# Two exponential tiles in one ScalarE instruction, 17 joint maximum units for 14, and six edits of the ending, in a fused attention and GEGLU kernel

## The chip, the cores and the metric

One core of a Trainium2 chip runs the whole program. The metric is the device time of one execution in microseconds (us); three runs of the kernel before gave 1225.08 us in the median (1224.64 to 1225.44). In the views, PE is TensorE (PEld its weight loads), DVE VectorE, ACT ScalarE, POOL GpSimd, and SP (SyncE) issues the DMAs.

## What is computed

A transformer block without masks on one sequence, inputs and output in bf16: S = 2048 tokens, D = 512 channels, H = 32 heads of 16 channels, and a feed-forward width F = 1792.

```python
def attn(x, wqkv, wo):
    q, k, v = split(x @ wqkv)                      # 32 heads of 16
    p = softmax(einsum("bhqd,bhkd->bhqk", q, k) * 16 ** -0.5)
    return merge(einsum("bhqk,bhkd->bhqd", p, v)) @ wo

def ffn(x, w_gate, w_up, w_down):
    return (gelu_tanh(x @ w_gate) * (x @ w_up)) @ w_down

h  = x + attn(layernorm(x), wqkv, wo)
h2 = h + ffn(layernorm(h), w_gate, w_up, w_down)   # the output
```

The softmax is over 32 x 2048 x 2048 scores, 134 million of them. Each must be seen twice: once for the maximum of its row, once for its exponential.

## The kernel before, in words

**Units and ticks.** The attention is cut into 64 units. A unit is 4 heads by 256 queries by all 2048 keys, and takes 16 ticks of the main loop. Each tick has a part of *pass 1* for one unit and a part of *pass 2* for the unit 24 ticks behind it (`P2_START`):

- Pass 1 (`p1_pair`, L852; `p1_consume`, L867 or L864): PE writes a pair of score tiles, 128 queries by 512 keys each, into two neighbouring PSUM banks; DVE takes the row maxima of both in one reduce. Four banks, 0 to 3, serve pass 1 as two pairs in turn, so a pair can be written again when the maximum of two ticks before has ended. At a unit's end POOL negates and splits the maxima, a transposing DMA turns them, and POOL adds them to the queries (L922), so that the scores of pass 2 come out with the maximum subtracted.
- Pass 2 (`p2_tile`, L943; `p2_consume`, L972): PE computes the scores again, transposed (keys by queries, 128 x 512 numbers a tile), two tiles a tick, and ACT takes the exponential of each into one of 34 SBUF slots. The slots lie in three tensors, PTM (23), PTE (4) and PTG (7), and are used in turn.

**The PSUM banks of pass 2.** Banks 4 to 7 are handed out by the class `Banks`: a list of free banks, from which `take` pops the first and to which `give` appends. A bank is given back as soon as the instruction that reads it has been planned, so the list is in the order of last use and `take` returns the bank whose reader is oldest. What still has to be awaited on the chip is settled by semaphores.

**Dense items.** All other matrix work is cut into items that run as Python generators: PV products (`item_pv`, L989, at the end of which L696 copies the 128x256 result to OB), projections, gate and up products, down products (`item_down`, L1391), and the difference tiles of the joint units. The class `Dense` lets one item run at a time. It holds one bank from its first piece to its last and yields between the pieces, so one piece is planned per tick, behind the two pass 2 tiles; where no piece fits, a dummy matmul (L1587) keeps PE going. The bank is given back when the item ends.

**Plan and order.** Nothing is scheduled by the hardware or by a compiler: `Plan` records each engine's instructions in program order and puts in semaphore waits from the reads and writes. `act_lag` is an estimate of how far ACT has fallen behind, to which each planned instruction adds; items start, and GELU polynomials and tanhs are placed, by that estimate and by another for POOL (`PoolStream`).

**The group.** In each tick the pass 1 pair and the first tile of pass 2 are wrapped in `group_begin` and `group_end`. The latter gathers the waits of all matmuls in between and puts them in front of the first one:

```python
        for i in range(i0, len(e.ops)):
            fn, waits, sig, dsem = e.ops[i]
            allw.extend(waits)
            e.ops[i] = (fn, [], sig, dsem)
```

So the pass 1 matmuls also wait for the reader of the bank that the first pass 2 tile is to take. The second tile stands outside the group and has its own wait.

**Joint units.** In 14 of the 64 units (`JOINT`) one tick of pass 1 is left out. For two heads, PE makes the difference of two key blocks' scores in one bank (`item_diff`: two accumulating matmuls), ACT writes its Relu to SBUF (L1080), and at tick 10 of the unit two DVE instructions (L864: add the Relu to the scores, take the row maximum) give the joint maximum of both blocks. At tick 14 the loop skips the tick (`J_GONE`); `behind` then counts the two pass 2 tiles that are owed, and the next two odd ticks take a third tile each (`more`).

**The ending.** Once pass 1 is over (`dve_free`), pass 2 runs in double exponentials (`p2_pair`, L960), two per pair of ticks, while the copies of dense items go to DVE. The last group of tokens has its own path: `item_oprojA` and `item_hnA` (output projection and second layer norm of its first half), `item_raw` (gate and up products of that half, copied raw), and `tail_b`, straight-line code for the last PV product, the norm, GELU, down products and the output DMA.

Of the kernel before, what the change touches and what calls it, by code (L numbers as in the profile page):

```python
# [209 lines left out]
ACT = mybir.ActivationFunctionType  # L210
# [5 lines left out]
NFC = F // 128  # L216
# [5 lines left out]
PV_T = (15, 16, 17, 18)  # L222
PV_TL = (9, 10, 17, 18)
DOWN_AT = 2
A_LATE = True
GH = 6
# [11 lines left out]
SLOPE = 0.02  # L238
JOINT = (5, 9, 12, 14, 17, 20, 25, 28, 33, 36, 41, 44, 49, 60)
J_AT, J_GONE = 10, 14  # L240
LAG_EXTRA = 0.3
POLY = 1.3
TICK = 1.135
# [4 lines left out]
def bass_sequential_preLN__mha_block__geglu_ffn__prompt_kernel(nc, A_x, A_wqkv, A_wo, B_x, B_w_gate, B_w_up, B_w_down, out):  # L248
    dbg = None
    with ExitStack() as es:  # L250
# [288 lines left out]
        class Dense:  # L539
            def __init__(self):  # L540
                self.prio = []
                self.ready = []
                self.extra = []
                self.gen = None
                self.bank = None
# [21 lines left out]
            def piece(self):  # L567
                if self.single and self.pause > 0:
                    return 0
                while True:  # L570
# [17 lines left out]
                    try:  # L588
                        cost = next(self.gen)
                        if isinstance(cost, tuple):  # L590
                            if self.single:
                                self.pause = cost[1]
                            if ticking[0]:
                                return 0
                            continue
                        return cost
                    except StopIteration as fin:
                        self.gen = None
                        self.done += 1
                        if self.single:  # L600
                            banks.give(self.bank)
                            self.pause = 0 if dve_free[0] else PAUSE
                        return fin.value
            def busy(self):
                return bool(self.gen is not None or self.ready or self.prio)
# [342 lines left out]
        def p2_pair(ui, tiles):  # L948
# [12 lines left out]
            else:  # L961
                for b, pi in ((b0, q0), (b1, q1)):
                    P.op("act", lambda e, b=b, pi=pi: e.activation(out=PTt(pi), in_=pbank[:, b, :], func=ACT.Exp), reads=[("pb", b)], writes=[("PT", pi)])

        def p2_consume(ui, tiles):
            for (b, m, g) in tiles:
                pi = pt_n[0] % NPT; pt_n[0] += 1
                assert pi not in pt_busy, "PT ring too small"
                pt_busy.add(pi)
                pt_of[(ui, m, g)] = pi  # L970
                dX = rdeps("M", [(n_, i_) for n_ in ("QKE", "QKE2") for i_ in range(5)]) if NPT_M - 10 <= pi < NPT_M else rdeps("E", [("xn", t) for t in range(NT)]) if NPT_M <= pi < NPT_M + NPT_E else (rdeps("G", [("x", cc) for cc in range(NCH)]) if pi >= NPT_M + NPT_E else ())
                P.op("act", lambda e, b=b, pi=pi: e.activation(out=PTt(pi), in_=pbank[:, b, :], func=ACT.Exp), reads=[("pb", b)], writes=[("PT", pi)], extra_deps=dX)  # L972
                banks.give(b)
# [216 lines left out]
        def item_oprojA(b):  # L1190
# [7 lines left out]
            P.op("pe", lambda e: e.matmul(pbank[:, b, :], ident[:], hh, start=False, stop=True), reads=["ident", ("h", GL % 2, 0)], writes=[("pb", b)], sig=True)  # L1198
            P.op("dve", lambda e: e.bn_stats(out=stats2[:, t, :], in_=pbank[:, b, :]), reads=[("pb", b)], writes=[("stats2", t)])
            P.op("dve", lambda e: e.tensor_copy(out=hh, in_=pbank[:, b, :]), reads=[("pb", b)], writes=[("h", GL % 2, 0)])  # L1200
            P.op("dve", lambda e: e.bn_aggr(out=mv2[:, t, :], in_=stats2[:, t, :]), reads=[("stats2", t)], writes=[("mv2", t)])
            P.op("dve", lambda e: e.tensor_scalar(out=rstd2[:, tt], in0=mv2[:, tt, 1], scalar1=EPS, scalar2=None, op0=ALU.add), reads=[("mv2", t)], writes=[("rstd2", t)])
# [7 lines left out]
        def item_hnA(b):  # L1210
            pt = pbank[:, b, :].bitcast(BF16)
            for dc in range(4):
                P.op("pe", lambda e, dc=dc: e.transpose(out=pt[:, 128 * dc:128 * dc + 128], in_=hn_sb[:, 0, 128 * dc:128 * dc + 128], identity=ident[:]),
                     reads=[("OH", 0), "ident"], writes=[("pb", b)], sig=(dc == 3))
            P.op("dve", lambda e: e.tensor_copy(out=hnT_l[GL % 2][:, :, 0:128], in_=pt[:, 0:512].rearrange("p (c s) -> p c s", c=4)), reads=[("pb", b)], writes=[("hnT", GL % 2, 0)])
            add_raw()
            return 1
            yield
# [299 lines left out]
        def tail_b():  # L1518
# [7 lines left out]
            for t in range(NTL):  # L1526
                raw_gelu(t)
            raw_mult(0)
            while not a_done[0]:
                fill(1)  # L1530
# [12 lines left out]
            P.op("pool", lambda e: e.tensor_tensor(out=rstd2[:, tt], in0=rstd2[:, tt], in1=nhalf[:, 0:1], op=ALU.pow), reads=[("rstd2", t1), "nhalf"], writes=[("rstd2", t1)])  # L1543
            raw_mult(1, "dve")
            raw_mult(2)
            raw_mult(3)
            P.op("dve", lambda e: e.tensor_scalar(out=hn_sb[:, 1, :], in0=g_h(GL, 1), scalar1=mv2[:, t1, 0:1], scalar2=rstd2[:, tt], op0=ALU.subtract, op1=ALU.mult),
                 reads=[("h", 1, 1), ("mv2", t1), ("rstd2", t1)], writes=[("OH", 1)])
            down_h(0, GL, 0)
            for fc in chunks(0):  # L1550
                down_mm(0, GL, 0, fc)
            fill(FILL_A)
            tail_hnT(2, (0, 1), "act")
            tail_hnT(3, (2, 3), "dve")
            for fc in chunks(1):
                down_mm(0, GL, 0, fc)
# [6 lines left out]
            for t in range(NTL):  # L1563
                tail_gate(gb[2 * t % 5], t)
                tail_up(gb[(2 * t + 1) % 5], t)
                if t == 0:
                    for fc in range(8, NFC):
                        down_mm(0, GL, 0, fc)
                    P.op("act", lambda e: e.activation(out=out_sb[:, 0, :], in_=pbank[:, 0, :], func=ACT.Copy), reads=[("pb", 0)], writes=[("osb", 0)])
                    P.dma("sp", lambda e: e.dma_start(out=outv[:, 2 * GL, :], in_=out_sb[:, 0, :]), ("out", 0), reads=[("osb", 0)], writes=[("outd", 2 * GL)])  # L1570
# [33 lines left out]
        ticking[0] = True  # L1604
        def next_tile():
            n = 2 * t2 - behind[0]
            st, jj = n // 2, n % 2
            ui_ = st // 16
            t = p2_tile(ui_, st % 16, 1 - (st + P2_START) % 2, jj)
            return ui_, t  # L1610
        while True:
# [62 lines left out]
            if t1:  # L1674
# [83 lines left out]
```

## Time and profile before

The page is of one profiled execution.

| | us |
|---|---|
| median of three runs | 1225.08 (1224.64 to 1225.44) |
| the profiled execution | 1225.74, its span 1224.0 |
| PE busy | 1130.3 (92%) |
| DVE busy | 1181.1 (96%), 1124 instructions |
| ACT busy | 1190.3 (97%), 2421 instructions |
| POOL busy | 841.3 (69%) |
| L867, maxima on DVE | 996 instructions, 1134.9 |
| L972, exponentials on ACT | 2000 instructions (PTM 1357, PTG 407, PTE 236), 1098.4 |
| L1587, dummy matmuls | 774, 237.0 |
| granted TensorE clock | full speed in all 40 slices |
| HBM read, written | 11.80 MB, 2.10 MB |

How to read it: an engine's busy time is the sum of its instructions' durations, and a duration can be longer than the distance to the next instruction of the same engine, since the end of one overlaps the start of the next. So the distance from start to start in an unbroken run is the price of an instruction, not its mean duration. A busy PE says little here: it runs dummies where it has nothing to do. A group's "idle before" is the time that its engine stood still just ahead of its instructions, with what ended most of it; in the page, the tile of a group is named by the program's names without numbers, so the banks are all "pbank".

In the views by window, a row has the stretch (us from the span's start), then the busy time of PE, of PEld with its count, of DVE, ACT and POOL, then the granted clock, the DMA share and the GB/s. In the chain of what ended last, a row has the start, the duration, the engine and the tile and line. In the time line, a row is one instruction with its start and duration, and in brackets the idle time of its engine ahead of it with what ended it.

### The profile page before, as it was taken

The numbers are of one execution on the slowest core, as the hardware profiler recorded it, in microseconds if no ns is written. First come the engines' busy times: TensorE is split into PE (matmuls) and PEld (weight loads), VectorE is DVE, ScalarE is ACT, GpSimd is POOL, SyncE is SP. The second block draws the span as 40 slices with busy tenths as digits, with TensorE's granted clock in tenths as the row PEclk, the third lists the DMA queues.
The fourth block names the chain that finished last, engine by engine and source line by source line (L and its number), as shares of the span: only waits on it lengthen the run. The fifth ranks groups of instructions, "written<-read, shape, count | busy, mean of one in ns | idle before, by whom it ended". The sixth has DMA issues, their size and how long they took to land.

```text
span 1224.0 us, 36091 instructions
## 1 busy us (share of the span) xinstructions
PE 1130.3 (92%) x14845; PEld 476.7 (39%) x14845; DVE 1181.1 (96%) x1124; ACT 1190.3 (97%) x2421; POOL 841.3 (69%) x1774
## 2 busy tenths in 40 slices
PE   7999998899999999999999999999999999999998
PEld 3233232233333333333332333333334455554565
DVE  8999999999999999999999999999999999999963
ACT  7899999999999999999999999999999999999995
POOL 8567684766776676756868487675767687756762
PEclk9999999999999999999999999999999999999999
DMA  5111104300010000110011000100001100010000
GB/s 153 28 34 27 29 24 136 91 10 9 8 28 21 12 11 8 27 25 8 11 25 14 21 8 10 25 21 15 8 10 27 26 20 13 10 27 13 18 20 15
DMA packets 69651, 32.02 MB, mean 26 GB/s; under 512 B 54768, under 2 KB 68464, under 8 KB 69488
## 3 DMA queue, kind: packets, MB, share of 16 engines
q1 hardware_dynamic: 69488, 29.71, 10.0%
q8 instruction: 118, 1.93, 0.7%
q14 instruction: 45, 0.37, 0.1%
HBM read 11.80 MB, written 2.10 MB: 11 GB/s over the span
## 4 chain that ended last, share of the span: by engine, by line
ACT 56%; DVE 32%; PE 8%; issue 2%; DMA 1%; POOL 1%; POOLq 0%; DVEq 0%
ACT PTM L972 32%; DVE PM L867 31%; ACT PTG L972 10%; ACT PTE L972 5%; PE pbank L1391 2%; ACT th_sb L1262 2%; ACT g_sb L696 2%; ACT u_sb L696 2%; PE pbank L943 1%; PE pbank L852 1%; ACT PTM L960 1%; ACT OB L696 1%; PE pbank L1292 1%; PE pbank L1587 1%; DVE OA L864 1%
## 5 line engine op out<-in xcount | busy, mean ns | idle before, releaser
L867 DVE TENSOR_REDUCE PM<-pbank 128x2 f32<-128x1024 f32 x996 | 1134.9, 1213 | 9.3 <-PE pbank L943 4.4
L972 ACT ACTIVATE PTM<-pbank 128x512 bf16<-128x512 f32 x1357 | 733.0, 718 | 4.4 <-PE pbank L943 1.0
L943 PE MATMUL pbank<-QT,KT 32*128 32x256 bf16 (+1 forms) x5120 | 506.2, 250 | 14.6 <-ACT PTM L972 8.1
L852 PE MATMUL pbank<-KT,QT 32*128 32x512 bf16 x2020 | 388.2, 384 | 25.4 <-DVE PM L867 10.0
L1587 PE MATMUL pbank<-ones_bf,ident 128*128 128x512 bf16 x774 | 237.0, 384 | 29.2 <-ACT PTM L972 4.7
L852 PEld LDWEIGHTS pbank<-KT,QT 32*128 32x128 bf16 x2020 | 97.2, 91 | 351.1 <-DVE PM L867 130.2
L943 PEld LDWEIGHTS pbank<-QT,KT 32*128 32x128 bf16 x5120 | 205.9, 92 | 69.0 <-ACT PTM L972 40.1
L972 ACT ACTIVATE PTG<-pbank 128x512 bf16<-128x512 f32 x407 | 225.1, 710 | 0.8 <-PE pbank L943 0.4
L972 ACT ACTIVATE PTE<-pbank 128x512 bf16<-128x512 f32 x236 | 140.3, 719 | 1.0 <-PE pbank L943 0.7
L989 PE MATMUL pbank<-PTM,VA 128*17 128x256 bf16 (+1 forms) x3470 | 126.0, 252 | 1.6
L1030 POOL TENSOR_TENSOR LINV<-OBT,negone 128x8 f32<-128x8 bf16 x63 | 105.1, 1668 | 6.2 <-DMA OBT<-OB 5.9
L1587 PEld LDWEIGHTS pbank<-ones_bf,ident 128*128 128x128 bf16 x774 | 45.3, 97 | 132.6 <-ACT PTM L972 83.8
L1272 POOL TENSOR_TENSOR th_sb<-g_sb 128x512 f32<-128x512 f32 (+1 forms) x50 | 51.2, 1024 | 63.6 <-ACT g_sb L696 63.6
L989 PEld LDWEIGHTS pbank<-PTM,VA 128*17 128x17 bf16 x3470 | 67.1, 90 | 39.8 <-issue 22.1
L1271 POOL TENSOR_TENSOR th_sb<-th_sb,g_sb 128x512 f32<-128x512 f32 (+1 forms) x50 | 62.4, 1248 | 4.0
L922 POOL TENSOR_TENSOR QT<-QT,STG 128x256 bf16<-128x256 bf16 x64 | 42.8, 668 | 31.8 <-DMA STG<-ST 31.1
L1274 POOL TENSOR_TENSOR th_sb<-th_sb,g_sb 128x512 f32<-128x512 f32 (+1 forms) x50 | 62.3, 1246 | 1.7
L1270 POOL TENSOR_SCALAR th_sb<-th_sb 128x512 f32<-128x512 f32 (+1 forms) x50 | 30.5, 611 | 40.9 <-ACT th_sb L1262 40.7
L1391 PE MATMUL pbank<-wd_sb,GUT 128*128 128x512 bf16 x210 | 57.4, 382 | 1.0 <-DVE OnT L1422 0.3
L767 POOL TENSOR_SCALAR QT<-QKS,qmask 128x512 bf16<-128x512 bf16 x30 | 46.9, 1568 | 13.3 <-ACT QKS L696 11.9
L1347 PE MATMUL pbank<-hnT_l,wg_sb 128*128 128x256 bf16 x336 | 51.2, 275 | 3.3 <-ACT PTM L972 0.7
L1383 POOL TENSOR_TENSOR GUT<-th_sb,u_sb 128x512 bf16<-128x512 f32 x42 | 53.3, 1268 | 1.3
(198 smaller groups left out, 1210.1 us busy)
## 6 DMA issues: line engine op xcount, KB each, us to landing
QKS<-QKS SPq DMA_DIRECT2D x27, 112.0 KB, 2.1
x_sb<-in_A_x_dram SPq DMA_DIRECT2D x4, 512.0 KB, 5.8
xres<-in_A_x_dram SPq DMA_DIRECT2D x16, 128.0 KB, 2.4
out_dram<-out_sb SPq DMA_DIRECT2D x15, 128.0 KB, 1.7
wg_sb<-in_B_w_gate_dram SPq DMA_DIRECT2D x4, 448.0 KB, 4.2
wu_sb<-in_B_w_up_dram SPq DMA_DIRECT2D x4, 448.0 KB, 3.9
wd_sb<-in_B_w_down_dram SPq DMA_DIRECT2D x3, 512.0 KB, 4.5
STG<-ST SPq DMA_TRANSPOSE x64, 2.3
```

Of the source, the lines that this page charges most:

```text
L696: P.op("act", lambda e: e.activation(out=o_ap, in_=i_ap, func=ACT.Copy, **kw), reads=reads, writes=writes, extra_deps=extra)
L852: P.op("pe", lambda e, g=g, b=b: e.matmul(pbank[:, b, :], QT[32 * g:32 * g + 32, c, slot, 128 * qt:128 * qt + 128], KT[32 * g:32 * g + 32, ...
L867: P.op("dve", lambda e: e.tensor_reduce(out=PM[:, par, qt, kc, g:g + 2], in_=pbank[:, b:b + 2, :], axis=AX.X, op=ALU.max), reads=[("pb", b ...
L943: P.op("pe", lambda e, kt=kt, i=i: e.matmul(pbank[:, b, qn * i:qn * i + qn], KT[32 * g:32 * g + 32, slot, 128 * kt:128 * kt + 128], QT[32 ...
L972: P.op("act", lambda e, b=b, pi=pi: e.activation(out=PTt(pi), in_=pbank[:, b, :], func=ACT.Exp), reads=[("pb", b)], writes=[("PT", pi)], e ...
L989: P.op("pe", lambda e, g=g, kt=kt, pi=pi, i=i, s_=s_, c0=c0, qn=qn: e.matmul(pbank[32 * g:32 * g + 17, b, c0:c0 + qn], VA[:, kt, 4 * s_ + ...
L1030: P.op("pool", lambda e: e.tensor_tensor(out=li, in0=o4[:, :, :, 16], in1=negone[:, 0:4 * nq].rearrange("p (q h) -> p q h", q=nq), op=ALU. ...
L1271: o(1.27, lambda e: e.tensor_tensor(out=ts_, in0=ts_, in1=gs, op=ALU.mult), [("th", par), ("g", par)])], then=done)
L1274: o(1.27, lambda e: e.tensor_tensor(out=ts_, in0=ts_, in1=gs, op=ALU.mult), [("th", par), ("g", par)])], then=poly_done)
L1383: P.op("pool", lambda e: e.tensor_tensor(out=o_ap, in0=shp(ts_), in1=shp(us), op=ALU.mult), reads=[("th", par), ("u", par)], writes=o_keys ...
L1391: P.op("pe", lambda e: e.matmul(pbank[:, b, :], GUT[:, fc, 128 * k:128 * k + 128], wd_sb[:, fc, :], start=first, stop=last), reads=[("GUT" ...
L1587: P.op("pe", lambda e: e.matmul(pbank[:, b, :], ident[:], ones_bf[:, 0:512], start=True, stop=True), reads=["ident", "ones_bf"], writes=[( ...
```

## The change

**In the loop.** Ahead of the group, `pair_banks` looks for the first bank in the free list whose neighbour (4 with 5, 6 with 7) is free as well. It is called only where pass 1 and pass 2 both run and no dense item holds a bank. If there is one, the two tiles of the tick go into these two banks, the lower one first, in place of the two banks at the head of the list. `p2_both` then makes one ACT instruction over both banks (1024 numbers a partition), if the next two slots are neighbours in the same SBUF tensor; if not, two single ones. A third tile is as before. Each pair takes 0.05 off the estimate `act_lag`.

**Joint units.** Units 22, 30 and 39 join the list.

**Around the end of the loop.** Once pass 1 is over (`dve_free`), an item that has to wait lets another one run beside it in a second bank (`beside`, `under`). Two of the four due times of the last unit's PV pieces go from 17 and 18 to 14 and 17 (counted from its first tick), one more dense piece is planned behind the loop (`TAIL_P`), the raw items are added a tick later, and the statistics of the first half of the last tokens are taken from the bf16 copy in SBUF, behind that copy, in place of PSUM.

**In `tail_b`.** Of the four products of raw gate and up, number 1 goes from DVE to POOL and ahead of the wait for the last attention output, number 2 from POOL to DVE, and number 3 from POOL to DVE behind the transposed copies. Of the 14 down products of the first half, 8 stand ahead of those copies in place of 4, then 4 in place of 4, and 2 in place of 6 behind the first gate and up products.

```diff
-PV_TL = (9, 10, 17, 18)
+PV_TL = (9, 10, 14, 17)
+TAIL_P = 1
-JOINT = (5, 9, 12, 14, 17, 20, 25, 28, 33, 36, 41, 44, 49, 60)
+JOINT = (5, 9, 12, 14, 17, 20, 22, 25, 28, 30, 33, 36, 39, 41, 44, 49, 60)
+PAIR_GAIN = 0.05
...
                         if isinstance(cost, tuple):
+                            if dve_free[0]:
+                                other_cost = self.beside()
+                                if other_cost:
+                                    return other_cost
...
+            def beside(self):
+                if self.under is None:
+                    if not self.ready or not banks.free or self.ready[0][3] > self.now or not startable(self.ready[0], 99):
+                        return 0
+                    genfn, a, est, nb = self.ready.pop(0)
+                    b = banks.take()
+                    self.under = (genfn(b, *a), b, genfn)
+                try:
+                    cost = next(self.under[0])
+                    return 0 if isinstance(cost, tuple) else cost
...
+        def pair_banks():
+            for b in banks.free:
+                if b ^ 1 in banks.free:
+                    return b & 6
+            return None
+
+        def p2_both(tl):
+            (ua, (b0, ma, ga)), (ub, (b1, mb, gb)) = tl
+            n = pt_n[0] % NPT
+            if n + 1 < NPT and pt_tiles[n][0] is pt_tiles[n + 1][0] and b1 == b0 + 1:
+                (q0, d0), (q1, d1) = place(ua, ma, ga), place(ub, mb, gb)
+                o_ap = pt_tiles[q0][0][:, pt_tiles[q0][1]:pt_tiles[q0][1] + 2, :]
+                P.op("act", lambda e: e.activation(out=o_ap, in_=pbank[:, b0:b0 + 2, :], func=ACT.Exp), reads=[("pb", b0), ("pb", b1)], writes=[("PT", q0), ("PT", q1)], extra_deps=d0 + d1)
+                banks.give(b0)
+                banks.give(b1)
+                act_lag[0] = max(0.0, act_lag[0] - PAIR_GAIN)
+            else:
+                for u_, t_ in tl:
+                    p2_consume(u_, [t_])
...
-            P.op("dve", lambda e: e.bn_stats(out=stats2[:, t, :], in_=pbank[:, b, :]), reads=[("pb", b)], writes=[("stats2", t)])
             P.op("dve", lambda e: e.tensor_copy(out=hh, in_=pbank[:, b, :]), reads=[("pb", b)], writes=[("h", GL % 2, 0)])
+            P.op("dve", lambda e: e.bn_stats(out=stats2[:, t, :], in_=hh), reads=[("h", GL % 2, 0)], writes=[("stats2", t)])
...
-            add_raw()
+            defer(1, add_raw)
...
             raw_mult(0)
+            raw_mult(1)
...
-            raw_mult(1, "dve")
-            raw_mult(2)
-            raw_mult(3)
+            raw_mult(2, "dve")
...
-            for fc in chunks(0):
+            for fc in range(8):
                 down_mm(0, GL, 0, fc)
...
             tail_hnT(3, (2, 3), "dve")
-            for fc in chunks(1):
+            raw_mult(3, "dve")
+            for fc in chunks(2):
                 down_mm(0, GL, 0, fc)
...
-                    for fc in range(8, NFC):
+                    for fc in chunks(3):
                         down_mm(0, GL, 0, fc)
...
-        def next_tile():
+        def next_tile(bank=None):
...
-            t2l = [next_tile()] if p2_ok and p1_ok else []
+            pb_ = pair_banks() if p2_ok and p1_ok and dense.gen is None and True else None
+            t2l = [next_tile(pb_)] if p2_ok and p1_ok else []
             P.group_end("pe")
             if p2_ok and p1_ok:
                 behind[0] -= 1
-                t2l.append(next_tile())
+                t2l.append(next_tile(None if pb_ is None else pb_ + 1))
...
+            if pb_ is not None:
+                p2_both(t2l[:2])
+                t2l = t2l[2:]
             for ui_, t in t2l:
                 p2_consume(ui_, [t])
...
+        for _ in range(TAIL_P):
+            dense.pause = 0
+            dense.piece()
```

The slots' bookkeeping of `p2_consume` (ring position, regions that have to be retired first) moves to a helper, `place`, unchanged.

More of the change, by code (lines that the diff above doesn't have):

```diff
@@ L544, in __init__ @@
                 self.gen = None
+                self.under = None
                 self.bank = None
@@ L599, in piece @@
                         self.done += 1
+                        ended = self.bank
+                        if self.under is not None:
+                            self.gen, self.bank, self.cur = self.under
+                            self.under = None
                         if self.single:
-                            banks.give(self.bank)
+                            banks.give(ended)
                             self.pause = 0 if dve_free[0] else PAUSE
                         return fin.value
+            def beside(self):
[8 more added lines that the diff above has]
+                    return 0 if isinstance(cost, tuple) else cost
+                except StopIteration as fin:
+                    banks.give(self.under[1])
+                    self.under = None
+                    return fin.value
             def busy(self):
@@ L963, in p2_pair, with place @@
                     P.op("act", lambda e, b=b, pi=pi: e.activation(out=PTt(pi), in_=pbank[:, b, :], func=ACT.Exp), reads=[("pb", b)], writes=[("PT", pi)])
+        def place(ui, m, g):
+            pi = pt_n[0] % NPT; pt_n[0] += 1
+            assert pi not in pt_busy, "PT ring too small"
+            pt_busy.add(pi)
+            pt_of[(ui, m, g)] = pi
+            dX = rdeps("M", [(n_, i_) for n_ in ("QKE", "QKE2") for i_ in range(5)]) if NPT_M - 10 <= pi < NPT_M else rdeps("E", [("xn", t) for t in range(NT)]) if NPT_M <= pi < NPT_M + NPT_E else (rdeps("G", [("x", cc) for cc in range(NCH)]) if pi >= NPT_M + NPT_E else ())
+            return pi, list(dX)
+        def pair_banks():
[16 more added lines that the diff above has]
+                    p2_consume(u_, [t_])
         def p2_consume(ui, tiles):
             for (b, m, g) in tiles:
[L967 to L971, printed above, removed]
+                pi, dX = place(ui, m, g)
                 P.op("act", lambda e, b=b, pi=pi: e.activation(out=PTt(pi), in_=pbank[:, b, :], func=ACT.Exp), reads=[("pb", b)], writes=[("PT", pi)], extra_deps=dX)
@@ L1608, in next_tile @@
             ui_ = st // 16
-            t = p2_tile(ui_, st % 16, 1 - (st + P2_START) % 2, jj)
+            if bank is not None:
+                banks.free.remove(bank)
+            t = p2_tile(ui_, st % 16, 1 - (st + P2_START) % 2, jj, bank)
             return ui_, t
```

## The prediction

> **What bounds the kernel now.** I read the page's busy times first, then the windows by 100 us, then the chain that ended last, then the time line of a few ticks. A tick is one pass of the main loop: one maximum on DVE, two exponentials on ACT.
>
> The page (columns: busy, share, instructions) and two of its groups:
> ```profile
> PE 1130.3 (92%) x14845; PEld 476.7 (39%) x14845; DVE 1181.1 (96%) x1124; ACT 1190.3 (97%) x2421; POOL 841.3 (69%) x1774
> ...
> L867 DVE TENSOR_REDUCE PM<-pbank 128x2 f32<-128x1024 f32 x996 | 1134.9, 1213 | 9.3 <-PE pbank L943 4.4
> L972 ACT ACTIVATE PTM<-pbank 128x512 bf16<-128x512 f32 x1357 | 733.0, 718 | 4.4 <-PE pbank L943 1.0
> ```
> One window of the middle (busy us of PE, PEld, DVE, ACT, POOL):
> ```profile
> 500.00:600.00 100.00, 93.15 (x1041) 34.25 (x1041) 99.61 (x91) 99.25 (x205) 70.14 (x161) 1.00 0.06 14
> ```
> DVE and ACT are both full. The chain of the ending changes hands between them, and its unbroken runs give each one's step:
> ```profile
> 645.74 34.01 DVE PM L867 x30
> 679.75 0.60 DVE OA L864
> 680.36 0.60 DVE OA L864
> ```
> ```profile
> 872.65 5.91 ACT PTM L972 x12
> ```
> ```profile
> 1198.09 3.67 ACT PTM L960 x4
> ```
> A maximum steps 34.01/30, less the last record's tail, 1.13 us; an exponential 5.91/12 = 0.49; a double one 3.67/4 = 0.92 (0.06 less than two singles). A joint step, two L864, takes 1.22 in place of two maxima, 2.26.
>
> What matters most here is how a tick hangs together where nobody is behind. Time line (start, duration):
> ```profile
> 1176.10 0.39 PE L852 MATMUL pbank<-KT,QT 32*128 32x512 bf16 x2
> ...
> 1176.53 1.23 DVE L867 TENSOR_REDUCE PM<-pbank 128x2 f32<-128x1024 f32 x1 [0.23 <-PE pbank L943]
> 1176.59 0.60 ACT L972 ACTIVATE PTE<-pbank 128x512 bf16<-128x512 f32 x1 [0.16 <-PE pbank L943]
> ...
> 1177.81 0.23 PEld L943 LDWEIGHTS pbank<-QT,KT 32*128 32x128 bf16 x8 [0.38 <-DVE PM L867]
> ```
> From the start of PE's group (G) the maximum starts after 0.43 and the first exponential after 0.49; an exponential alone takes 0.60, a double one alone 1.04 (mean 1074 ns over 15, less for the undisturbed). The maximum ends at 1177.76 and PE goes on at 1177.81: a release costs 0.05. The maxima need a group every 1.13. A group may start when the maximum two ticks back has ended, so it can be early by 1.13 - 0.08 (records overlap) - 0.05 - 0.43 = **0.57 us of slack**; what is later than that stops DVE. Two groups stand as close as 0.87 here:
> ```profile
> 500.94 0.39 PE L852 MATMUL pbank<-KT,QT 32*128 32x512 bf16 x2
> ...
> 501.81 0.39 PE L852 MATMUL pbank<-KT,QT 32*128 32x512 bf16 x2
> ```
> so 0.26 of lost slack comes back in a tick.
>
> **The change, part by part.**
>
> *Double exponentials.* In the built program's order 540 L972 pairs of the loop become one instruction each: 540 x 0.06 = 34 us less work for ACT. What this can give is capped by DVE: 996 x 1.13, 14 joint steps x 1.22 and some 3.5 us of early statistics fill all but 15 us between its first maximum (14.9) and its last (1177.8). Some 1.7 of these lie before 36 us, 1.0 at 895 behind a transposing DMA; 11.5 remain that a quicker ACT could remove (ends: 0 and 13).
>
> *Three more joint units.* 3 x (2.26 - 1.22) = 3.1 us less on DVE, and 6 Relus x 0.49 = 2.9 more on ACT.
>
> *The banks.* Before, the two tiles of a tick take the oldest free banks. Now, where no item holds a bank, `pair_banks` takes the first free bank **together with its neighbour, however recently that was used**. The wait of the first tile stands in front of the whole PE group (`group_end` moves it there), so the two P1 matmuls behind it, and through them DVE, wait for ACT as well. Counting in the built order which ACT instruction each of these groups waits for: before, at least two newer ones always stand behind it (313 times two, 274 three, five four; else a wait already met). After, 265 have one, and **134 wait for the newest of all**: ACT then runs empty while PE fills banks. 62 of them follow the tick "exp, exp, OB" (end of a unit's product, L696), 33 a difference tile's Relu (L1080), 33 a third tile's exponential in a joint unit, 6 others. A difference tile shows why: at its tick it takes the oldest bank, 4, and gives it back; the next pair takes the now oldest, 5, and with it 4.
>
> The price of such a tick, group to group: ACT start 0.49 + double 1.04 + Relu or third tile 0.49 + release 0.05 = 2.07; with OB 0.49 + 0.60 + 0.49 + 0.28 + 0.05 = 1.91. Against 1.13, with full slack, DVE loses 2.07 - 1.13 - 0.57 = 0.37 and 1.91 - 1.13 - 0.57 = 0.21; with none left 0.94. Two ticks after another such one: ACT 0.49 + 1.04 + 0.92 + 0.49, release 0.05, makes 2.99 against 2.26: 0.73. Four after: between 0.27 and 0.84, by whether slack is left; I take 0.55. By their distances in the order: 62 x 0.21 = 13.0; 20 directly behind another x 0.94 = 18.8; 21 two behind x 0.73 = 15.3; 18 four behind x 0.55 = 9.9; 7 apart and 6 others x 0.37 = 4.8. **Sum 62 us.** Ends: 134 all apart, 40; all but OB without slack, 81. Such a stretch is not in the trace of before; the nearest rows are those above.
>
> A second count, by ACT alone: from 66 to 1177.6 us its instructions, each at its step, make 1093 of 1112 us. After: 1093 - 33 + 3 = 1063; each empty stretch costs 0.05 + 0.49 + 0.12 (a double one alone against in a row) = 0.66, and 125 of them lie there: 82, so 1145. Thus 33 us longer even if ACT never idled otherwise. The truth lies above, as ordinary ticks (0.92 of 1.13) idle too.
>
> *The ending.* 24 double exponentials stay, 1178.0 to 1201.8; a half tanh (0.3) leaves them, and idle 0.40 and 0.48 before two may shrink as two L685 copies leave DVE. Then:
> ```profile
> 1203.30 0.29 DVE L685 COPY OA<-pbank 128x128 f32<-128x128 f32 x1 [0.33 <-PE pbank L989]
> ...
> 1207.87 1.27 DVE L1547 TENSOR_SCALAR OnT<-xres,mv,rstd 128x512 bf16<-128x512 bf16 x1 [0.52 <-POOL rstd L1543]
> ```
> The last product no longer stands behind the down item: the OA copy comes some 1.0 earlier. But POOL's second L1490 now stands ahead of its pow, to 1203.87 + 2 x 1.27 = 1206.41 (before: pow from 1206.82), so only 0.4 survives. L1547 ran beside L1490 on POOL; its twin L1204, alone, took 0.41, so 0.86 is gained. PE then does 9 down products (0.22 each) in place of 4 ahead of the gate, and 2 in place of 6 later: 0.4 lost, with the moved residual product. Net 0.9, and 0.4 from the stretch before: 1.3 (ends 0 and 3). The output's DMA on SP follows the same instructions. The swap of L1199 and L1200, the tick's delay of the raw items and the delayed tail items are covered by these doubles on ACT; uncovered they are some 0.7 us. BN from bf16 SBUF adds nothing (L395, 0.68, against 0.70).
>
> *Sum.* Against the profiled execution, 1225.74 us (span 1224.0): - 3.1 - 11.5 - 1.3 + 62 = +46, so 1271.8. The median shown is 0.66 below the profiled one: **1271 us**.
>
> **The rivals.**
> 1. The forecast, 1271: chance 0.72.
> 2. The waits lose only what each loses alone, 40 us, and all old stalls go (13), the ending gives 3: 1225 - 3 - 13 - 3 + 40 = 1246. For it: old stalls and new ones may fall together. Against: 41 of 72 waits of the joint units stand one or two ticks behind another. Chance 0.14.
> 3. **Faster**: the waits find ACT ahead and cost nothing, and DVE alone sets the pace: 1225.1 - 3.1 - 11.5 - 1.3 = 1209. Place: the 134 groups; it decides below 16/134 = 0.12 us for each. For it: ACT has 34 us less to do, and both engines share the chain now. Against: ACT cannot be ahead of tiles that wait for its newest instruction. But the slack is read from one undisturbed tick, and one half larger would cover the most frequent kind. Chance 0.12.
>    [...]
> 4. The change hardly pairs (rings and banks seldom fit) and little moves: 1224, within 0.2%. The built order shows the 540 doubles; chance 0.02.
>
> [...]
>
> **How the numbers follow.** Low end: rival 2, less 6 us if other slack meets a sixth of its 40, 1240. High end: all 72 without slack, 68, OB 13, old stalls halved: 1225 - 3 - 6 + 81 + 1 = 1298. Faster by over 0.2% (about what a measurement here can tell from no change) 0.12, within 0.02, slower 0.86.
>
> **What would show it.** DVE's idle before L892 (now L867) far above 9.3, released by PE; waits of the P1 weight load (L877) for ACT, on instructions of the new double line, OB and OA, in place of those for DVE; ACT busy well below 97%; 990 maxima and 34 joint steps; joint units longer than plain ones by some 2 to 3 us. Wrong, if DVE's busy share in the middle stays at 99%: then rival 3. If the groups of L877 do wait and DVE doesn't, the slack is mis-sized.

## The result and the profile after

The changed kernel takes **1404.34 us** in the median (1399.46 to 1406.66, 4 runs) against 1225.26 before: a ratio of 1.145, 95% interval 1.1435 to 1.1469. It is slower by 179 us, where 46 were forecast. The profiled execution took 1404.33 us, its span 1402.6.

The page of the changed kernel, the rows that answer to those of before (busy times, the granted clock by slices, and the maxima and exponentials with the idle time ahead of them):
```profile
PE 1124.8 (80%) x14694; PEld 463.1 (33%) x14840; DVE 1205.2 (86%) x1128; ACT 1224.5 (87%) x1890; POOL 844.0 (60%) x1779
...
PEclk9999999989999999899988999999999999999999
...
L892 DVE TENSOR_REDUCE PM<-pbank 128x2 f32<-128x1024 f32 x990 | 1155.6, 1218 | 164.0 <-PE pbank L968 157.7
...
L1010 ACT ACTIVATE PTM<-pbank 128x1024 bf16<-128x1024 f32 x398 | 395.8, 1023 | 73.4 <-PE pbank L968 67.1
L1021 ACT ACTIVATE PTM<-pbank 128x512 bf16<-128x512 f32 x561 | 310.7, 597 | 33.8 <-PE pbank L968 31.6
```
The maxima waited 9.3 us before and 164.0 now, nearly all for PE. ACT, full before, waits for PE as well, and PE itself fell from 92% to 80%. Three engines wait for one another, and none is full. Here is the same window of the middle as before:
```profile
500.00:600.00 100.00, 80.61 (x897) 28.38 (x905) 85.33 (x76) 85.85 (x132) 62.55 (x136) 0.90 0.06 14
```
DVE does 76 instructions in it in place of 91, ACT is busy 85.85 in place of 99.25, and the granted clock is 0.90 where it was 1.00.

What PE's pass 1 group waits for, in the waits of the changed kernel (us in total, times, longest):
```profile
PEld pbank L877 <- ACT PTM L1021: 89.2, 137, 1.5
...
PEld pbank L877 <- ACT OB L721: 69.2, 62, 1.6
...
PEld pbank L877 <- ACT OA L1129: 34.9, 33, 1.2
PEld pbank L877 <- ACT PTG L1021: 32.0, 50, 1.4
...
PEld pbank L877 <- ACT PTE L1021: 18.0, 30, 1.6
```
The 62 waits for OB and the 33 for a difference's Relu (written to OA) are the ones that the prediction counted, to the number. Of the 217 behind a single exponential (137, 50 and 30, by the tensor that it writes) it had priced only the 33 third tiles of the joint units.

Laid out along DVE's records: from the first maximum to the end of the last 1162.8 us before and 1342.9 now, so the loop lost 180.1; from there to the end 46.2 before and 44.9 now. Of the 180.1, 154.8 are more idle time ahead of maxima; the rest is mainly the 0.08 us by which two records in a row overlap, lost at 311 more maxima (25), less the 3.1 of the joint units.

### The profile page after: what moved, and what is told of

Read it like the earlier page. It is cut to its first block, busy times and chain, and to the rows that moved or that the text cites. A ratio compares the mean times of both kernels' runs of the same rounds, so it can differ in the third digit from the quotient of the medians.

```text
span 1402.6 us, 35383 instructions
## 1 busy us (share of the span) xinstructions
PE 1124.8 (80%) x14694; PEld 463.1 (33%) x14840; DVE 1205.2 (86%) x1128; ACT 1224.5 (87%) x1890; POOL 844.0 (60%) x1779
## 4 chain that ended last, share of the span: by engine, by line
ACT 58%; PE 35%; issue 3%; DVE 3%; DMA 0%; POOL 0%
ACT PTM L1010 19%; ACT PTM L1021 15%; PE pbank L968 10%; PE pbank L877 10%; ACT PTG L1021 6%; ACT PTG L1010 5%; PE pbank L1636 5%; ACT PTE L1021 4%; PE pbank L1038 3%; PE pbank L1440 3%; ACT PTE L1010 2%; PE pbank L1396 2%; DVE PM L892 2%; ACT th_sb L1311 2%; ACT OB L721 1%
## 5 line engine op out<-in xcount | busy, mean ns | idle before, releaser
L892 DVE TENSOR_REDUCE PM<-pbank 128x2 f32<-128x1024 f32 x990 | 1155.6, 1218 | 164.0 <-PE pbank L968 157.7
L877 PE MATMUL pbank<-KT,QT 32*128 32x512 bf16 x2014 | 401.4, 399 | 150.7 <-ACT OB L721 53.0
L1010 ACT ACTIVATE PTM<-pbank 128x1024 bf16<-128x1024 f32 x398 | 395.8, 1023 | 73.4 <-PE pbank L968 67.1
L1021 ACT ACTIVATE PTM<-pbank 128x512 bf16<-128x512 f32 x561 | 310.7, 597 | 33.8 <-PE pbank L968 31.6
L1636 PE MATMUL pbank<-ones_bf,ident 128*128 128x512 bf16 x650 | 218.0, 406 | 44.5 <-ACT PTM L1010 23.6
L968 PEld LDWEIGHTS pbank<-QT,KT 32*128 32x128 bf16 x5120 | 189.5, 93 | 110.7 <-ACT PTM L1010 60.6
L1010 ACT ACTIVATE PTG<-pbank 128x1024 bf16<-128x1024 f32 x102 | 102.8, 1025 | 22.7 <-PE pbank L968 20.7
L1021 ACT ACTIVATE PTG<-pbank 128x512 bf16<-128x512 f32 x203 | 113.6, 598 | 6.3 <-PE pbank L968 5.7
L1321 POOL TENSOR_TENSOR th_sb<-g_sb 128x512 f32<-128x512 f32 (+1 forms) x50 | 51.2, 1024 | 97.7 <-ACT g_sb L721 97.7
L1021 ACT ACTIVATE PTE<-pbank 128x512 bf16<-128x512 f32 x156 | 89.1, 599 | 7.7 <-PE pbank L968 7.2
L920 POOL TENSOR_TENSOR MX<-PM,MX 128x8 f32<-128x8 f32 x64 | 12.9, 202 | 82.5 <-DVE PM L892 81.7
```

What stands on the lines that cost most here:

```text
L877: P.op("pe", lambda e, g=g, b=b: e.matmul(pbank[:, b, :], QT[32 * g:32 * g + 32, c, slot, 128 * qt:128 * qt + 128], KT[32 * g:32 * g + 32, ...
L892: P.op("dve", lambda e: e.tensor_reduce(out=PM[:, par, qt, kc, g:g + 2], in_=pbank[:, b:b + 2, :], axis=AX.X, op=ALU.max), reads=[("pb", b ...
L968: P.op("pe", lambda e, kt=kt, i=i: e.matmul(pbank[:, b, qn * i:qn * i + qn], KT[32 * g:32 * g + 32, slot, 128 * kt:128 * kt + 128], QT[32 ...
L1010: P.op("act", lambda e: e.activation(out=o_ap, in_=pbank[:, b0:b0 + 2, :], func=ACT.Exp), reads=[("pb", b0), ("pb", b1)], writes=[("PT", q ...
L1321: pool.add([o(1.04, lambda e: e.tensor_tensor(out=ts_, in0=gs, in1=gs, op=ALU.mult), [("g", par)], dE), o(0.62, lambda e: e.tensor_scalar( ...
L1636: P.op("pe", lambda e: e.matmul(pbank[:, b, :], ident[:], ones_bf[:, 0:512], start=True, stop=True), reads=["ident", "ones_bf"], writes=[( ...
```

## The experiments

All are told as changes to the changed kernel, unless said otherwise. Where no interval stands, the time is of one run.

**e1, no pairs, 14 joint units.**
```diff
+JOINT = (5, 9, 12, 14, 17, 20, 25, 28, 33, 36, 41, 44, 49, 60)
...
-            pb_ = pair_banks() if p2_ok and p1_ok and dense.gen is None and True else None
+            pb_ = None
```


> The changed kernel with pairing switched off and the joint list back at 14: only the edits around the ending and the due times stay. The pairs theory (all of the loss lies in the loop, the ending gained its 1.3 us: 46.2 us from the last maximum to the end before, 44.9 after): 1223.9 us, within 0.5. Rival, the ending or its edits lose part of the 179: clearly above 1226.

Measured 1224.27 us, ratio 0.9988 (0.9979 to 0.9997), and 44.9 us after the last maximum. So the edits of the ending are worth some 1 us, as predicted, and all of the loss comes with the pairs and the three units.

**e2, the same banks, but single exponentials.**
```diff
-            if n + 1 < NPT and pt_tiles[n][0] is pt_tiles[n + 1][0] and b1 == b0 + 1:
+            if False:
```
(The 0.05 is still taken off `act_lag`, so that all other work keeps its place.)

> The changed kernel with the same choice of banks and the same order of all work, but two single exponentials wherever it made a double one. Theory A (the bank choice: 134 groups wait for ACT's newest instruction, at 0.78 us each): these waits stay, 105 us, and only what the late release by a double costs goes (59 us of groups that wait for one op with one newer, 28 of groups held up behind a second tile): about 1320 us, 1290 to 1345. Theory B (the double instruction itself, which gives both banks back late): the loss is nearly gone, 1225 to 1245.

Measured 1372.56 us, above the range of theory A. Theory B falls: without one double in the loop 147 of the 179 us stay. Theory A is right in kind but too low; the granted clock was 0.96 here too, of which more at e13.

**e3, no pair on the bank that was given back last.**
```diff
             for b in banks.free:
-                if b ^ 1 in banks.free:
+                if b ^ 1 in banks.free and banks.free[-1] not in (b, b ^ 1):
```


> The changed kernel, but a pair never holds the bank that was given back last. 540 doubles as before; no group waits for ACT's newest instruction, 409 wait for one with one newer (265 in the changed kernel), and 210 second tiles still wait for the newest. Theory A: the 105 us of the 134 groups go, and some of them return as waits with one newer (at 0 to 0.39 us each): 1300 to 1355 us, 1325 most likely. Theory B: the doubles are all there, so nearly nothing changes, 1380 to 1410.

Measured 1322.37 us, as theory A said, with all 540 doubles.
```profile
L892 DVE TENSOR_REDUCE PM<-pbank 128x2 f32<-128x1024 f32 x990 | 1151.0, 1218 | 87.6 <-PE pbank L968 81.0
```
Of the 87.6 us that its maxima still wait, 75.9 stand in the ticks whose group waits for an instruction with one newer behind it. That is what the prediction had left out. The granted clock was 0.996, so a part of the gain can be the clock's (e13).

**e4, no group.** The first tile is taken out of the group:
```diff
-            t2l = [next_tile(pb_)] if p2_ok and p1_ok else []
             P.group_end("pe")
+            t2l = [next_tile(pb_)] if p2_ok and p1_ok else []
```


> The changed kernel with the first tile of pass 2 taken out of the group: the two pass 1 matmuls wait for DVE alone, and the tile behind them waits for ACT by itself. Bank choice and doubles as in the changed kernel; 346 tiles wait for the newest ACT instruction. Theory A with the hoisted wait as the link to DVE: each maximum gets its scores one wait earlier, a whole tick of 1.13 us more slack, and DVE's idle time of 164 us falls under 40: 1230 to 1270 us, 1245 most likely. Rival (ACT running empty is the bound, wherever the wait stands): over 1330.

Measured 1379.74 us: the rival. Only 25 us go, and the granted clock was 0.975 in place of 0.96, so a part of them can be the clock's. The hoisted wait is not the main link. ACT still runs empty: up to the end of the loop its gaps sum to 142 us here, to 164 in the changed kernel.

**e5, one kind of wait alone.** In e1, the tick behind a PV product takes the bank just given back:
```diff
+            ob_ = banks.free[-1] if p2_ok and p1_ok and dense.gen is None and dense.done > done_[0] and dense.cur is item_pv and banks.free[-1] == dense.bank else None
+            done_[0] = dense.done
-            t2l = [next_tile(pb_)] if p2_ok and p1_ok else []
+            t2l = [next_tile(ob_)] if p2_ok and p1_ok else []
```


> No pairs, 14 joint units, as e1 (1224.27 us), with one thing added: in the tick behind the end of a PV product the first tile takes the bank that OB has just given back. That makes 62 groups wait for ACT's newest instruction, nothing else changes, and every exponential is single. By the prediction's price (0.21 us each, since 0.57 of slack takes up the rest): 13 us, 1237. Theory C (ACT, at 99% in the middle, has nothing with which to win the slack back in the 15 ticks between, so a wait costs 1.91 - 1.13 = 0.78 until ACT's reserve of some 19 us is spent): 48 - 19 = 29, 1253 us, up to 1270.

Measured 1259.38 us: 35 us for 62 waits, 0.57 each, where the prediction had 0.21. Theory C stands.

**e6 and e7, the same with a quarter less to do for ACT.** From the fifth unit on (`ui >= 4`) an exponential leaves out the last 128 of its 512 columns, in e1 (e6) and in e5 (e7):
```diff
-                P.op("act", lambda e, b=b, pi=pi: e.activation(out=PTt(pi), in_=pbank[:, b, :], func=ACT.Exp), reads=[("pb", b)], writes=[("PT", pi)], extra_deps=dX)
+                w_ = 384 if ui >= 4 else 512
+                P.op("act", lambda e, b=b, pi=pi, w_=w_: e.activation(out=PTt(pi)[:, 0:w_], in_=pbank[:, b, 0:w_], func=ACT.Exp), reads=[("pb", b)], writes=[("PT", pi)], extra_deps=dX)
```


> As e1, but from the fifth unit on each exponential takes 384 of its 512 columns (it leaves out a quarter of each tile; the rest of the slot keeps old numbers): ACT has some 0.2 us less to do per tick, DVE and PE the same work. The base for e7. Both theories: DVE sets the pace, 1213 to 1224 us.

> e5 and e6 together (a quarter of each exponential tile left out from the fifth unit on): the same 62 groups wait for ACT's newest instruction, but ACT has 0.2 us of spare time in each of the ticks between. Group to group in such a tick is then 1.91 - 2 x 0.107 = 1.70. Theory C: the slack of 0.57 is back each time, 1.70 - 1.13 - 0.57 = 0, so at most 5 us above e6. Rival D (a wait that empties ACT has a fixed price, for the restart of the engines or the lower PE clock): 62 x 0.57 = 35 us above e6.

Measured 1211.71 (e6, just below the range) and 1218.78 us (e7): the 62 waits now cost 7 us, not 35. Two rows each of e5 and of e7 say it (the maxima on the page; what the group waits for):
```profile
L892 DVE TENSOR_REDUCE PM<-pbank 128x2 f32<-128x1024 f32 x996 | 1139.0, 1216 | 38.7 <-PE pbank L968 33.7
```
```profile
PEld pbank L877 <- ACT OB L721: 70.7, 62, 1.6
```
```profile
L892 DVE TENSOR_REDUCE PM<-pbank 128x2 f32<-128x1024 f32 x996 | 1133.3, 1216 | 4.7 <-PE pbank L968 1.9
```
```profile
PEld pbank L877 <- ACT OB L721: 61.7, 62, 1.2
```
PE stands nearly as long at the same 62 places (70.7 and 61.7 us), but DVE waits 38.7 us in the one and 4.7 in the other. With the spare time on ACT, PE is early enough at the next such place. Not all of the difference is returned slack, though: of the 0.46 us by which a wait became cheaper (0.57 to 0.11), 0.21 is, by an estimate, that the tick itself is shorter (1.70 in place of 1.91, two exponentials at 0.107 less; in e10 one of 384 columns alone takes 0.49, where one of 512 takes 0.60). The other 0.25 is then slack that is there again.

**e8, pairs only on the two oldest banks.**
```diff
-            for b in banks.free:
-                if b ^ 1 in banks.free:
-                    return b & 6
-            return None
+            f = banks.free
+            return f[0] & 6 if len(f) > 1 and f[0] ^ 1 == f[1] else None
```
Besides, where no bank is left for a dummy matmul, this kernel makes none.

> The changed kernel (17 joint units, the new ending), but a pair is made only where the two oldest free banks are neighbours in the right order, so that no tile gets a younger bank than it would without pairs. 152 doubles stay of 540; no group waits for the newest ACT instruction, 48 for one with one newer, all of them behind a double (which cost nothing in the changed kernel), and 65 second tiles wait for the newest, where a single follows a double. Theory A and C: 1225 - 1.3 - 3.1 + 65 x (0.08 to 0.25) = 1226 to 1237. Theory B (each double costs, by its late release): 179 x 152/540 = 50, 1270.

Measured 1255.61 us, ratio 1.0246 (1.0228 to 1.0264), outside what theory A and C gave. The loop itself did as they said: its last maximum ended 11.8 us later than before. But in this plan the dense items fell behind, and the ending took 65.3 us in place of 44.9. One tile of the last group but one even takes its down product from products of gate and up that are overwritten by then, so this kernel's output is wrong; the amount of work is the same. So the pairs that cost little are also few (152), and in the loop they win nothing.

**e9, two kinds of wait.** As e5, with `dense.cur in (item_pv, item_diff)`.

> As e5 (1259.38 us), and the tick behind a difference tile also takes the bank that the Relu has just given back: 28 more groups wait for ACT's newest instruction, 90 in all, no doubles. Theory C: the reserve is spent by the 62 already, so each new one costs in full, 0.49 + 0.60 + 2 x 0.49 + 0.05 - 1.13 = 0.99 us less what was left (6 us): 22 to 28 us more, 1281 to 1287. By the prediction's price (0.37 each, 0.55 to 0.94 where another is near): 10 to 18 us more, 1270 to 1277.

Measured 1294.74 us: 35 us more than e5 for 28 waits, more than either. The waits themselves cost 0.84 idle and 0.08 of lost overlap, 26 us together, as theory C had it. The other 9 stand beside a granted clock of 0.979, where e5 had 1.0.

**e10, the changed kernel with narrow exponentials.** The edit of e6, in both forms of the exponential.

> The changed kernel itself, with all its pairs, waits and 17 joint units, but from the fifth unit on each exponential takes 384 of its 512 columns per tile (a quarter of each tile is left out). ACT then has 0.2 us of spare time in most ticks. To be compared with e6 (1211.71 us). Theory C: the slack is back between most waits; only the joint units' ones that stand close together still cost: 20 to 40 us, so 1228 to 1249. Rival D (fixed price for each wait, less the shorter exponentials inside it): 179 - 282 x 0.21 = 120 us, 1330.

Measured 1293.49 us, 82 above e6: between the two. The OB kind fell from 0.50 idle each to 0.09, the waits with one newer from 47.3 us to 11.1, as theory C says. Most of the joint units' waits stayed (37 us idle of 59). They stand one to four ticks behind one another; that this is too close for slack to return is the likely reason, but no run separates it. And 36 ticks under half the clock lost 17.

**e11, 14 joint units with the pairs.**

> The changed kernel with the joint list back at 14 units. 119 groups wait for ACT's newest instruction in place of 134. Each unit less saves two difference tiles' and two third tiles' waits (five waits a unit by the count, near 0.9 us) and gives back 1.04 us of DVE: 1404 - 15 x 0.9 + 3 = 1394 us, 1388 to 1400.

Measured 1384.61 us, below the range. The three units cost 20 us, 6.6 each, where DVE's own records give a gain of 1.04 each. That is more than expected; the clock was 0.974 in place of 0.96, so a part of it is the clock's, and how much is open.

**e12, e3 without the group.** The edits of e3 and e4 together.

> e3 (1322.37 us: no pair on the bank given back last) with the first tile of pass 2 taken out of the group as in e4. 540 doubles; no tile of the group waits for the newest, 210 second tiles do. Theory C: the bound is ACT running empty or nearly so behind waits with one newer instruction, not the hoist; as e4 won 25 of 179, this wins some 10 to 30 of 97: 1292 to 1312. Rival (with ACT not wholly emptied, the hoisted wait is all that holds DVE up): 1225 to 1250.

Measured 1310.28 us: 12 us won, as theory C said. It stays 86 us behind e1.

**e13, PE kept busy ahead of the waits.**
```diff
+            if p1_ok and p2_started and dense.gen is None:
+                nb_ = pair_banks()
+                if nb_ is not None and banks.free[-1] & 6 == nb_:
+                    dummy(banks.free[0], 3)
             run_deferred(tick)
```


> The changed kernel with three dummy matmuls (0.22 us each in a row) put behind the last piece of every tick whose successor's pair holds the bank given back last, so that PE computes while it would otherwise stand idle ahead of the 134 groups (its mean idle time there is 0.85 to 0.91 us, so they fit in). Waits, banks and doubles are unchanged. Theory E (a part of the loss is the granted clock, which stood at half for 21 stretches of the changed kernel; 67 ticks there lost 0.63 us each, against 0.15 in the others): the clock stays at or above 0.99 and 67 x 0.48 = 32 us go, 1372 us, 1362 to 1382. Rival (the half clock stands where PE has nothing to do anyway and costs nothing): 1400 to 1408.

Measured 1379.56 us at a granted clock of 0.999: 25 us go, for 405 matmuls more (the four runs of the changed kernel lie within 7.2 us). Theory E stands, a little smaller than expected.
```profile
L892 DVE TENSOR_REDUCE PM<-pbank 128x2 f32<-128x1024 f32 x990 | 1151.8, 1219 | 143.0 <-PE pbank L968 136.2
```
The maxima wait 143.0 us in place of 164.0. These are windows of the changed kernel, around its longest stretch under half the clock (the columns as in the windows before; the clock is the third number from the right):
```profile
726.00:728.00 2.00, 1.77 (x12) 0.55 (x12) 1.92 (x2) 1.64 (x3) 1.78 (x4) 1.00 0.00 0
728.00:730.00 2.00, 1.05 (x8) 0.40 (x8) 0.91 (x2) 0.98 (x3) 1.45 (x8) 0.80 0.00 0
730.00:732.00 2.00, 2.00 (x11) 0.54 (x10) 1.29 (x2) 1.09 (x2) 1.85 (x5) 0.50 0.04 9
732.00:734.00 2.00, 1.32 (x8) 0.14 (x6) 0.67 (x1) 1.43 (x2) 2.00 (x2) 0.50 0.12 24
...
744.00:746.00 2.00, 2.00 (x32) 0.73 (x28) 1.71 (x2) 1.48 (x3) 0.65 (x3) 0.50 0.00 0
746.00:748.00 2.00, 2.00 (x48) 0.93 (x44) 1.50 (x3) 1.43 (x3) 0.00 (x0) 0.93 0.03 8
```
PE was half idle for 2 us (1.05 of 2.00), the clock fell to 0.50 for 17.1 us by its record, and in the windows wholly under it DVE did 0.67 to 1.71 of 2.00, while PE reads as busy for 1.32 to 2.00: its matmuls take longer (one of pass 1 has 0.60 us under half the clock, 0.38 else).

## Why the prediction was wrong

**What held.** The mechanism and its places: 134 groups behind ACT's newest instruction, found in the built order, are in the trace at 62, 33 and the rest, and e3, in which no group waits for the newest (409 wait with one newer in place of 265), wins 82 us. The doubles' own gain (0.92 in a row), the 990 maxima and 34 joint steps, and the signs to look for were right. Rival 3, which named the same 134 places and asked 0.12 us of each, is refuted.

The ending is right to the tenth (1.3), but that is in part luck. Counted from the last maximum, the last exponential ends 0.17 earlier than before, where 0.4 was forecast, and the normalisation (L1547, now L1595) 1.45 earlier, as it takes 0.41 in place of 1.27. Then the first gate-times-up product of the second half comes only 0.12 earlier, and the second 1.0. The shares differ from the forecast; their sum agrees.

**The step that failed** is "The price of such a tick": "with full slack, DVE loses ... 1.91 - 1.13 - 0.57 = 0.21". The 0.57 us of slack was read from one tick at 1176.10, where ACT had just stood idle (0.16), its return of 0.26 a tick from one pair of groups, and both were taken to hold everywhere. ACT had no time for that: its steps made 1093 of 1112 us, by the prediction's own second count, so after each wait the next groups are held back by ACT, and little of the slack is there when the next wait comes. The OB wait costs 0.57 (e5) and with spare time on ACT 0.11 (e7 less e6). In the trace of the changed kernel:
```profile
507.12 1.09 ACT L1021 ACTIVATE PTG<-pbank 128x512 bf16<-128x512 f32 x2
508.08 0.41 ACT L721 ACTIVATE OB<-pbank 128x256 bf16<-128x256 f32 x1
...
508.54 0.39 PE L877 MATMUL pbank<-KT,QT 32*128 32x512 bf16 x2 [1.32 <-ACT OB L721]
...
508.97 2.36 DVE L892 TENSOR_REDUCE PM<-pbank 128x2 f32<-128x1024 f32 x2 [0.88 <-PE pbank L968]
509.05 1.94 ACT L1010 ACTIVATE PTG<-pbank 128x1024 bf16<-128x1024 f32 x2 [0.57 <-PE pbank L968]
```
ACT ends OB at 508.49; 0.05 later PE starts its group, DVE its maximum at 508.97 and ACT its double at 509.05. PE, ACT and DVE take turns, where each should run beside the others. The last group had started at 506.13 with a tanh still ahead on ACT, so group to group took 2.41, not 1.91.

**The term put at nothing**: the 265 groups that wait for an instruction with one newer behind it. In 116 of them the one newer is a double exponential; these are free indeed (0.6 us in all). In 148 the order on ACT is "exp, exp, copy of a dense item", the group waits for the second exponential, and they cost 0.31 idle each. That exponential belongs to the tick just before. So the prediction's own way of counting gives a price, ACT start 0.49 + two exponentials 1.09 + release 0.05 = 1.63 from group to group, 0.50 over 1.13. Only with the full 0.57 of slack is that nothing: this term fails with the same slack.
```profile
510.67 0.39 PE L877 MATMUL pbank<-KT,QT 32*128 32x512 bf16 x2
...
511.04 0.11 PEld L968 LDWEIGHTS pbank<-QT,KT 32*128 32x128 bf16 x2 [0.26 <-ACT PTG L1010]
511.15 1.08 ACT L1021 ACTIVATE PTM<-pbank 128x512 bf16<-128x512 f32 x2 [0.15 <-PE pbank L968]
...
512.28 0.09 PEld L877 LDWEIGHTS pbank<-KT,QT 32*128 32x128 bf16 x2 [0.59 <-ACT PTM L1021]
...
512.72 1.23 DVE L892 TENSOR_REDUCE PM<-pbank 128x2 f32<-128x1024 f32 x1 [0.26 <-PE pbank L968]
```
The two singles start 0.48 behind the group, and the next group waits for the second of them: 512.28 - 510.67 = 1.61 from group to group, and DVE stands for 0.26. The second tile of the tick also waits here (0.26 us for the double that gives its bank back), but that is not what costs: of the 148 groups, counted in the built order and followed in the trace, 125 stand behind such a second tile and 23 don't, and both kinds cost 0.31 each. In e2, where nothing is double, the same 148 groups cost 0.20; why less is open.

**The clock** was not weighed at all. In the trace of before it is 1.00 throughout, and the prediction took it as given. In the changed kernel it stood at half in 21 stretches; the maxima and joint instructions of DVE under it lost 0.63 us each (67 of them, 42 us) and the others 0.16 (957, 152 us, of which 14 were lost before as well). Windows wholly inside a stretch show 0.50, those outside 1.00. The pauses of PE are short: from 60 us to the end of the loop none is over 1.33 us.

By the clock's record all 21 stretches begin and end on one grid with intervals of 3.41 us; they last one, two or five intervals. In the interval right ahead of a stretch PE was busy for 36 to 71%, worked out from its records (1% of which are missing). Of those 21 intervals 16 are below 61%; of the 340 others of the loop at full clock only 7 are. In e5, with 62 of the waits, no span of that length is below 55%, and the clock never falls. So the emptiest intervals are the ones that half the clock follows, but PE's busy share of the interval doesn't separate the two kinds entirely.

**The sum, term by term**, with the 0.08 of lost overlap added to each stall, at full clock (e13):

| term | predicted | measured |
|---|---|---|
| 134 groups, newest instruction | +62 | 90.2 + 134 x 0.08 = +101 |
| 265 groups, one newer | 0 | 43.1 + 149 x 0.08 = +55 |
| half clock | 0 | +25 (changed kernel less e13) |
| old stalls | -11.5 | -1: 14 before, 13 now, in other ticks |
| three joint units, DVE's own steps | -3.1 | -3.1 |
| ending | -1.3 | -1.3 |
| sum | +46 | +176, of 179 |

Within the first row, OB measures 0.58 each (0.21 predicted), the Relu 0.91 and the third tile 0.95 (0.37 to 0.94 predicted): near the price with no slack left (0.94) for the joint units' waits, and between the price with full slack and the one with none (0.78) for OB. The prediction's high end had "all 72 without slack" but kept OB at full slack and the other two terms at nothing, so it stopped at 1298.

Of the 25 us of the half clock, 16 stand in ticks whose group has none of these waits (they lose 30 us in the changed kernel and 13 in e13), and 8 in ticks that have one.

The old stalls were to give 11.5 us, and gave 1. The 11.5 doesn't follow from the prediction's own figures either: 996 x 1.13, 14 x 1.22 and 3.5 make 1146.1 of the 1162.9 us, which leaves 16.8 and not 15, and 14.1 less the 1.7 and 1.0.

What stays open: e13 also moves the ticks, so these 16 and 8 are no exact split; after which pauses of PE the clock halves is not settled, since intervals with 51 to 71% of busy time stand on both sides; and so is why the old stalls came back in other ticks.

No version here that computes the whole of the work beats the kernel before by more than e1 does, 0.12%.

## What to carry to other kernels

DVE and ACT were both at 99% in the middle of the kernel before, and slack read from one undisturbed tick was not there when it was needed: most of the length of a wait for ACT's newest instruction counted (0.57 of 0.78 us in e5), and little of it where ACT had spare time between two such waits (0.11 in e7). So count the whole length, until a row shows such spare time. A bank taken in place of the oldest, to have it beside its neighbour, cost more here than the merged instruction gave (0.06 us, against 0.6 to 0.95). Count, in the built order, what stands behind each awaited instruction, and ask whether the awaited one belongs to the tick just before: with a whole double behind it the wait cost nothing here, with one copy behind it 0.31. When waits take PE from 92% busy towards 80%, ask what the granted clock will do (0.96 here, 1.00 before); dummies ahead of the waits gave 25 us back here.

## What the hardware showed that was not expected

- The granted clock halved in 21 stretches of 3.4 to 17.1 us, in which a 512-column matmul of pass 1 took 0.60 us in place of 0.38. All begin and end on a grid of 3.41 us. No pause of PE is over 1.33 us from 60 us to the end of the loop.
- PE's busy share over the whole run does not tell it. e3 had 84% and a clock of 0.996, e9 88% and 0.979; e13, with 85%, 0.999. In e13 no interval of the 3.41 us grid from 60 us on is below 69%; in the changed kernel 21 intervals of 36 to 71% were followed by half the clock.
- With nearly the same wait on PE (70.7 us in e5, 61.7 in e7), DVE's maxima stood idle for 38.7 us in e5 and 4.7 in e7.
